# Spreading the first batch's 16 dense units over the second batch's attention steps

## The chip, the cores and the metric

The kernel runs on one core of a Trainium2 chip. The metric is device time in microseconds (us) of one execution. The engines of the core are named as in the profile: PE is the matrix engine, DVE the vector engine, ACT the activation engine, POOL the GpSimd engine, SP the engine whose queue issues nearly all DMAs; each runs its own instructions in the order in which the program lists them.

## The reference

Three stages follow one another. B is 4 batches, H 8 heads, S 576 positions, D 64.

```python
q_rot, k_rot = rotate(q), rotate(k)                    # rotary embedding
scores = q_rot @ k_rot.T / sqrt(D);  attn = softmax(scores)
x = (attn @ v)  -> [2304 tokens, 512]                  # stage 1
h = x @ w_in;  g = maximum(0.01 * h, h);  x2 = g @ w_out   # stage 2, d_ff = 2048
e = argmax_e(cos(x2, expert_emb) / tau)                # stage 3, 8 experts
out = gate * (relu(x2 @ w1[e]) @ w2[e])                # d_ff of an expert = 1024
```

Stage 2 needs whole rows of x, thus all eight heads of a token, and stage 3 needs x2 of all tokens before the last of its blocks can be formed.

## The kernel before, in words

Attention is done in 144 *steps*: 16 groups g (a batch and a pair of heads; four groups make a batch) of nine units u (128 queries of one head; the ninth takes the last 64 queries of both heads). Step i handles unit i: `a_max` (L574, DVE) reads the scores S of unit i and writes E, `a_exp` (L579, ACT) and `a_hi`/`a_lo` (L583 ACT, L587 DVE) follow for unit i-1, a DMA transposes the result P into PT, `a_pv` (L622, PE) multiplies it with v four steps later, `a_fin` (L640 to L644, DVE) normalizes, and `a_scores(i+1)` (L565, L567, L569, PE) makes the next scores. The scores have one buffer, so the scores of step i+1 wait for `a_max` of step i. Groups 0 to 3 (steps 0 to 35, batch 0) use another form in fp32.

The dense stage 2 is cut into 72 *units* in ten blocks of 256 tokens (two blocks hold 128). A unit of a 256-token block is 24 matmuls h<-x,wi (`m_s1`, L251), then on ACT and DVE `m_g` (L258), `m_leaky` (L261), `m_gh` (L265), `m_gl` (L269), then 12 matmuls into acc (`m_s2`, L281). Blocks 0 and 1 are the first 512 tokens of batch 0 and take 16 units; blocks 2 and 3 are those of batch 1, block 4 is the rest of batches 0 and 1, and so on. A block may begin once its rows have been scaled, split into two fp16 halves and transposed by DMA (`x_done`, L669 to L680). When a block's last unit has been added up, `m_out` (L293, L295) writes x2 and `route` follows for each 128 rows: a store by SP (L310), a sum of squares (L322), four transposes (L326), a copy (L329), eight small matmuls (L333) and one DVE operation (L335).

The order of all instructions is written out by hand in `step`. It walks through a string of letters; what belongs to the change:

```python
for z in ORDER_W if whole else ORDER1 if ... else ORDER_B if second else ORDER_A:
ORDER_A = 'ESXFHshLlVxsC'
ORDER_B = 'GXEKFHs2LVxsCo'
```

`S` is `m_s1` and stands only in ORDER_A, so a unit can begin only in a step of that form. If a unit was begun, or one is still between its two matmul parts, `M.second` is set and the following step takes ORDER_B, which holds the unit's `m_g` and `m_leaky` (`G`, `K`) and the `m_s2` of the unit before (`2`). `h` and `l` of ORDER_A are `m_gh` and `m_gl`. Without a pause the steps alternate A, B, A, B, and one unit begins in every second step: begun in step s, its second part stands in step s+3. `m_ready` says whether the next unit's rows and weights are there; then the unit begins as early as the order allows. `s` and `x` are slots into which background jobs (preparing the next groups, `x_done`, `route`, decoding of the weights) are put by a budget; the dense units are not counted in it.

After step 148 the attention is over; the units that are left run without attention steps, and the expert stage follows.

Of the kernel before, what the change touches and what calls it, by code (L numbers as in the profile page):

```python
# [40 lines left out]
EARLY = 2  # L41
TLOAD = 4
BUR = 1.5
ORDER_W = 'HXtEFVCsTsxs'
ORDER1 = 'HXEsFVsLsxCs'
ORDER_A = 'ESXFHshLlVxsC'
# [49 lines left out]
def attention_moe_kernel(ctx: ExitStack, tc: tile.TileContext, qkv, w_in, w_out, emb, tau, w1, w2,  # L96
# [30 lines left out]
    def ps_h():  # L127
        return psH.tile([128, 512], F32, name="h")
# [22 lines left out]
    munits = []  # L151
# [13 lines left out]
    M = Ctx()  # L165
# [5 lines left out]
    M.wdone = [set(), set()]  # L171
    M.scaled = set()
    M.step, M.tick = -1, 0
    block_of = {z: j for j, bl in enumerate(blocks) for z in bl}
    xjobs, vjobs, rjobs, wjobs = deque(), deque(), deque(), []

# [56 lines left out]
    def m_ready():  # L233
        if M.unit == len(munits):
            return False
        j, fs = munits[M.unit]
        return j < M.ready and all(f in w for f, _, _ in fs for w in M.wdone)

    def m_s1():

        if not m_ready():
            return None
        j, fs = munits[M.unit]
        M.unit += 1
        m = Ctx()
        m.j, m.fs, m.h = j, fs, ps_h()
        for f, c0, c1 in fs:
            n = 0
            for a, b_ in ((0, 0), (1, 0), (0, 1)):
                for c in range(4):  # L250
                    nc.tensor.matmul(m.h[:, c0:c1], lhsT=wi[:, a, c, 128 * f:128 * f + 128], rhs=xT[j][:, 4 * b_ + c, 0:c1 - c0],  # L251
                                     start=(n == 0), stop=(n == 11))
                    n += 1
        return m
# [808 lines left out]
    def step(i):  # L1063
# [4 lines left out]
        for e in budget:  # L1068
            budget[e] = min(budget[e] + rate[e], BUR * rate[e])
        now = i is not None and 0 <= i < n  # L1070
# [5 lines left out]
        second = M.second  # L1076
        for z in ORDER_W if whole else ORDER1 if rate is RATE1 and (turned or not m_ready()) else ORDER_B if second else ORDER_A:
            if z == "E" and whole:
# [5 lines left out]
            elif z == "t" and turned:  # L1084
                a_turned_end(*end_)
            elif z == "S":
                m = m_s1()
                M.second = bool(m or M.g or M.s)
                if m:
# [55 lines left out]
    for i in range(n + LAG + 1):  # L1145
# [4 lines left out]
        j = i - LAG - 1  # L1150
# [223 lines left out]
```

## Time and profile before

| | us |
|---|---|
| median of 3 runs | 1034.22 (1034.07 to 1034.79) |
| the profiled execution, its own time | 1036.97 |
| span from first to last instruction | 1035.2 |
| PE / DVE / ACT busy in the span | 943.6 / 776.9 / 672.0 |
| mean granted PE clock | 0.939 |

Busy shares over the whole span hide stages: the fp32 attention of batch 0 lies up to about 200 us, attention with dense units from there to about 640 us, the remaining dense units to about 762 us, and the experts after that. A gap in brackets behind a PE row is idle time before it, with what ended it.

### The profile page before, as it was taken

Reading aid. Unit: us, or ns where it says so; the run is one execution under the profiler, and the core shown is the slowest. Engines: PE = TensorE matmul, PEld = TensorE weight load, DVE = VectorE, ACT = ScalarE, POOL = GpSimd, SP = SyncE. Lnnn points to the kernel's source line nnn. Section 1 sums busy time; section 2 is a strip of 40 time slices with the busy share of each in tenths; the row PEclk is TensorE's granted clock in tenths of the full one; section 3 lists DMA queues with packets and bytes.
Section 4 is the critical chain, followed back from the end, with each engine's and each line's share of the span. In section 5 each row is a group of like instructions: output and inputs, shape, how many; then the busy total and the mean of one; then the engine's idle time right before and its main releaser. Section 6 shows DMA issues by size and latency. Waiting matters only on the chain. (4 is left out here: it accounts for less than half of the span.)

```text
span 1035.2 us, 19847 instructions
## 1 busy us (share of the span) xinstructions
PE 943.6 (91%) x7259; PEld 778.5 (75%) x7259; DVE 776.9 (75%) x1632; ACT 672.0 (65%) x1081; POOL 64.2 (6%) x64
## 2 busy tenths in 40 slices
PE   2577897999999689999899999999999999999996
PEld 1466786767787578888778888888877788888884
DVE  5776776878878878887987967422566999899992
ACT  5666666775655765765775655423255898888882
POOL 0000000000000000000000000000000452111110
PEclk9977656599999899999999999999999999999998
DMA  6334245385886787788687666200333111116190
GB/s 203 118 111 131 73 130 159 58 161 90 145 168 134 150 173 121 133 169 154 139 167 160 109 122 97 60 1 22 103 112 123 41 52 52 41 41 204 58 333 20
DMA packets 223623, 120.08 MB, mean 116 GB/s; under 512 B 194711, under 2 KB 204439, under 8 KB 223520
## 3 DMA queue, kind: packets, MB, share of 16 engines
q1 hardware_dynamic: 220320, 108.79, 45.5%
q0 software_dynamic: 3200, 9.97, 2.8%
q8 instruction: 59, 0.97, 0.4%
q14 instruction: 44, 0.36, 0.1%
HBM read 120.04 MB, written 10.49 MB: 126 GB/s over the span
## 5 line engine op out<-in xcount | busy, mean ns | idle before, releaser
L251 PEld LDWEIGHTS <-wi 128*128 128x128 f16 x1920 | 171.8, 99 | 27.1 <-issue 6.6
L281 PE MATMUL acc<-wo,gh 128*128 128x512 f32 x576 | 152.3, 406 | 2.7 <-ACT gh L265 2.7
L579 ACT ACTIVATE E<-E,amx 128x576 f32<-128x576 f32 x144 | 110.6, 768 | 32.4 <-DVE E L574 32.1
L258 ACT ACTIVATE g<-h 128x512 f32<-128x512 f32 x72 | 43.0, 598 | 133.8 <-PE h L251 57.1
L281 PEld LDWEIGHTS acc<-wo,gh 128*128 128x128 f32 x576 | 103.7, 189 | 26.4 <-ACT gh L265 4.7
L574 DVE TENSOR_SCALAR_CACHE_REDUCE E<-S,sc 128x576 f32<-128x576 f32 x108 | 87.8, 813 | 41.8 <-PE S L567 27.8
L251 PE MATMUL h<-xT,wi 128*128 128x256 f16 (+1 forms) x1152 | 113.5, 257 | 0.0
L587 DVE SCALAR_TENSOR_TENSOR P<-E,P 128x576 f16<-128x576 f32 x108 | 81.2, 752 | 17.4 <-ACT P L583 17.1
L583 ACT ACTIVATE P<-E 128x576 f16<-128x576 f32 x108 | 73.9, 684 | 31.4 <-DMA PT<-P 28.3
L251 PE MATMUL h<-xt,wi 128*128 128x256 f16 x768 | 90.8, 276 | 2.3 <-DMA xt<-x 2.3
L622 PEld LDWEIGHTS <-PT 128*128 128x128 f16 (+1 forms) x1680 | 61.1, 100 | 24.6 <-issue 14.7
L281 PE MATMUL acc<-wo,gl 128*128 128x512 f32 x288 | 77.9, 392 | 0.0
L622 PE MATMUL o<-v,PT 128*128 128x65 f16 (+3 forms) x1680 | 69.7, 194 | 6.5 <-DMA PT<-P 6.5
L261 DVE SCALAR_TENSOR_TENSOR g<-h,g 128x512 f32<-128x512 f32 x72 | 49.5, 688 | 29.2 <-ACT g L258 29.1
L565 PE MATMUL S<-stk 128*128 128x288 f16 (+1 forms) x240 | 60.9, 293 | 9.9 <-DVE E L574 9.8
L269 DVE TENSOR_TENSOR gl<-g,gh 128x512 fp32r<-128x512 f32 x72 | 49.4, 686 | 24.3 <-ACT gh L265 14.5
L622 PE MATMUL o<-v,ET 128*128 128x65 f32 (+1 forms) x400 | 64.5, 328 | 0.0
L281 PEld LDWEIGHTS acc<-wo,gl 128*128 128x128 f32 x288 | 54.7, 190 | 12.2
L622 PEld LDWEIGHTS o<-v,ET 128*128 128x128 f32 (+1 forms) x400 | 62.3, 246 | 0.7 <-issue 0.7
L989 PE MATMUL h<-w,hth 128*128 128x512 f32 x176 | 55.2, 395 | 0.4 <-ACT hth L973 0.4
L265 ACT ACTIVATE gh<-g 128x512 fp32r<-128x512 f32 x72 | 44.5, 618 | 15.1 <-PE acc L281 14.2
L550 PE MATMUL S<-qk 64*128 64x288 f32 (+1 forms) x96 | 38.5, 616 | 17.2 <-DVE ET L608 14.4
(255 smaller groups left out, 1957.5 us busy)
## 6 DMA issues: line engine op xcount, KB each, us to landing
rb<-in_w SPq DMA_DIRECT2D x78, 512.0 KB
ra<-in_w SPq DMA_DIRECT2D x76, 512.0 KB
raw<-in_qkv SPq DMA_DIRECT2D x15, 640.0 KB
raw<-in_w_in SPq DMA_DIRECT2D x16, 512.0 KB
raw<-in_w_out SPq DMA_DIRECT2D x16, 512.0 KB
x2s<-x SPq DMA_DIRECT2D x18, 256.0 KB
raw<-in_qkv SPq DMA_DIRECT2D x14, 320.0 KB
v<-v SPq DMA_DIRECT2D x12, 162.5 KB
```

The lines of the kernel that those rows point to most:

```text
L251: nc.tensor.matmul(m.h[:, c0:c1], lhsT=wi[:, a, c, 128 * f:128 * f + 128], rhs=xT[j][:, 4 * b_ + c, 0:c1 - c0], start=(n == 0), stop=(n == ...
L261: nc.vector.scalar_tensor_tensor(out=m.g, in0=m.h, scalar=0.01, in1=m.g, op0=ALU.mult, op1=ALU.max)
L265: nc.scalar.activation(out=m.gh, in_=m.g, func=AF.Copy)
L269: nc.vector.tensor_tensor(out=m.gl, in0=m.g, in1=m.gh.bitcast(F32), op=ALU.subtract)
L281: nc.tensor.matmul(M.acc[:, t], lhsT=g_[:, tt], rhs=wo[:, a, f], start=(f == 0 and n == 0), stop=(f == NF - 1 and n == 2))
L565: nc.tensor.matmul(ps[o:o + m, n, 0:288], lhsT=stk[:, h, c0:c0 + m], rhs=stk[:, 2 + h, ks], start=True, stop=False)
L574: nc.vector.tensor_scalar(out=e[:, 0:S].rearrange("p (a b) -> p a b", a=2), in0=ps[:, :, 0:288], scalar1=-0.125 if g < WHOLE else pairs[g] ...
L579: nc.scalar.activation(out=e[:, 0:S], in_=e[:, 0:S], func=AF.Exp, scale=-1.0, bias=mx)
L583: nc.scalar.activation(out=p[:, 0:576], in_=e[:, 0:S], func=AF.Copy, scale=TWO15)
L587: nc.vector.scalar_tensor_tensor(out=p[:, 576:1152], in0=e[:, 0:S], scalar=TWO15, in1=p[:, 0:576], op0=ALU.mult, op1=ALU.subtract)
L622: nc.tensor.matmul(o[ob:ob + m, 256 * h:256 * h + w], lhsT=pt[:, i, q0:q0 + m], rhs=v[:, j, h, c:c + w], start=(n == 0), stop=(n == len(to ...
L989: nc.tensor.matmul(OP[kk], lhsT=h_[:, c, :], rhs=wt[a][c // 2][:, 512 * (c % 2):512 * (c % 2) + 512], start=(n == 0), stop=(n == len(todo) ...
```

## The change

The diff gives the first batch's units a schedule. `M.first` is 16, the number of units of blocks 0 and 1. `M.begin` holds the step in which unit 0 begins. Until step 76, unit k is let through only once k (76 - begin) is no more than 16 (step - begin). Unit 16, the first of batch 1, is held to step 76 by the same line. From step 76 on nothing is held.

```diff
+NEXT = 76
...
+    M.first = sum(j < 2 for j, _ in munits)
...
         j, fs = munits[M.unit]
+        if not M.unit:
+            M.begin = M.step
+        if M.step < NEXT and M.unit * (NEXT - M.begin) > M.first * (M.step - M.begin):
+            return None
         M.unit += 1
```

No instruction is added or removed; only the order in the queues changes.

## Rows read from the trace of the kernel before

**Rows 1.** Windows: stretch, length, busy (count) of PE, PEld, DVE, ACT, POOL, clock, DMA.
```profile
203.60:244.79 41.19, 40.12 (x330) 29.06 (x329) 33.45 (x79) 27.05 (x46) 0.12 (x1) 0.97 0.72 124
244.79:296.31 51.52, 51.52 (x492) 41.06 (x492) 41.49 (x98) 31.67 (x55) 0.23 (x2) 1.00 0.68 131
296.31:334.06 37.75, 37.38 (x380) 30.95 (x378) 31.87 (x74) 22.25 (x38) 0.12 (x1) 1.00 0.79 160
334.06:370.55 36.49, 25.47 (x256) 20.35 (x257) 29.12 (x81) 26.29 (x50) 0.12 (x1) 0.86 0.76 154
370.55:384.71 14.16, 11.27 (x101) 8.93 (x100) 9.92 (x22) 7.53 (x14) 0.00 (x0) 0.88 0.89 208
384.71:640.00 255.29, 248.03 (x2600) 208.84 (x2598) 208.43 (x496) 164.35 (x282) 0.70 (x6) 1.00 0.74 137
640.00:762.00 122.00, 121.91 (x1006) 103.65 (x1005) 52.43 (x140) 42.94 (x77) 2.22 (x2) 1.00 0.22 62
```
**Rows 2.** L574 up to 355.1 us: count, ns min/median/max, first and last start.
```profile
L574 DVE TENSOR_SCALAR_CACHE_REDUCE E<-S,sc x38: 687/816/821, 199.8 to 351.3; 128x576 f32<-128x576 f32 x38
```
**Rows 3.** L251 from 199.5 to 334.0 us, same columns.
```profile
L251 PE MATMUL h<-xT,wi x384: 272/273/421, 202.6 to 329.2; 128*128 128x256 f16 x192
```
**Rows 4.** Timeline of PE (start, duration): start of the dense work, a regular pair, routing.
```profile
202.65 4.26 PE L251 MATMUL h<-xT,wi 128*128 128x256 f16 x24
...
218.98 2.79 PE L251 MATMUL h<-xT,wi 128*128 128x256 f16 x24
221.61 0.58 PE L622 MATMUL o<-v,PT 128*128 128x65 f16 x14
...
222.93 2.11 PE L281 MATMUL acc<-wo,gh 128*128 128x512 f32 x8
...
225.78 0.59 PE L622 MATMUL o<-v,PT 128*128 128x65 f16 x14
...
290.58 0.66 PE L326 MATMUL t<-idn,x 128*128 128x128 f32 x4
294.73 1.04 PE L333 MATMUL t<-enT,x2T 128*128 128x8 f32 x8
```
**Rows 5.** Timeline of PE from 336 to 380 us: three gaps and a slow row.
```profile
336.11 0.59 PE L622 MATMUL o<-v,PT 128*128 128x65 f16 x14 [2.09 <-DMA PT<-P]
...
355.19 4.45 PE L251 MATMUL h<-xt,wi 128*128 128x256 f16 x24 [2.25 <-DMA xt<-x]
...
378.62 0.28 PE L565 MATMUL S<-stk 128*128 128x288 f16 x1 [2.89 <-DVE E L574]
...
379.02 3.14 PE L281 MATMUL acc<-wo,gh 128*128 128x512 f32 x8
```
**Rows 6.** Windows around these gaps in which the clock fell, columns as in the first group.
```profile
345.00:353.00 8.00, 4.36 (x35) 3.21 (x32) 7.79 (x22) 5.66 (x12) 0.00 (x0) 0.57 0.56 107
353.00:360.00 7.00, 4.80 (x39) 3.73 (x39) 5.04 (x13) 4.72 (x9) 0.00 (x0) 0.76 0.54 109
...
378.00:385.00 7.00, 6.38 (x42) 4.86 (x42) 6.41 (x16) 5.26 (x11) 0.00 (x0) 0.76 0.79 178
```
**Rows 7.** DVE groups 203.6 to 334.06 us: count, busy, mean ns, idle before, releasers.
```profile
L574 DVE TENSOR_SCALAR_CACHE_REDUCE E<-S,sc 128x576 f32<-128x576 f32 x33 | 26.7, 810 | 19.1 <-PE S L569 12.9 <-PE S L567 5.9
L261 DVE SCALAR_TENSOR_TENSOR g<-h,g 128x512 f32<-128x512 f32 x16 | 11.0, 687 | 0.0
L269 DVE TENSOR_TENSOR gl<-g,gh 128x512 fp32r<-128x512 f32 x15 | 10.3, 684 | 0.0
```
**Rows 8.** Waits from 334.06 to 384.71 us: total, times, longest.
```profile
ACT x L674 <- DMA xt<-x: 4.9, 1, 4.9
DVE x L676 <- ACT x L674: 3.7, 1, 3.7
```
**Rows 9.** Timeline of SP: the two stores of block 1.
```profile
348.27 0.58 SPq L310 DMA_DIRECT2D x2s<-x  x1
...
368.13 0.46 SPq L310 DMA_DIRECT2D x2s<-x  x1
```

## The prediction, made before the result was known

> **What bounds the kernel now.** I read the windows first, cut where a_max of steps 37, 47, 59, 69, 77 and 80 starts, because a share over the whole span mixes stages. In the first three windows PE is busy 40.12 of 41.19, 51.52 of 51.52 and 37.38 of 37.75 us, at a clock of 0.97 to 1.00; DVE has 80 to 84% of the time [rows 1]. PE bounds there, and the DVE groups say the same from the other side: a_max waited 19.1 us in all for the scores from PE [rows 7]. In the fourth window (steps 69 to 76) PE is busy 25.47 of 36.49 us at 0.86, and in the fifth 11.27 of 14.16 at 0.88. From 384.71 to 640 us it is busy 248.03 of 255.29, and from 640 to 762 us, where only dense units are left, 121.91 of 122 [rows 1].
>
> Why the fourth window is empty is seen by counting. The first a_max with the tile sc belongs to step 36. 38 of them start up to 355.1 us, the last at 351.3, so that is step 73 [rows 2]. Unit 0 stands between the scores of steps 37 and 38: it begins in step 37, at 202.65 us [rows 4]. By 334 us, 384 matmuls of L251 have run, 24 each, so all 16 units [rows 3]: one in every second step, the last in step 67. Unit 16 starts at 355.19, in step 74, and waits 2.25 us for its rows even then [rows 5]. Between, steps 69 to 73 hold only the last second part (step 70).
>
> **The change part by part.** Nothing is added or removed: the sum is of moves. With begin 37, unit k is let through from step 37 + 39k/16 on, and it must also meet a step of form A. After a unit, A is every second step, and a refused A step is still followed by a B step, since the unit before is between its parts. So units keep to odd steps: 37, then 41, 43, 45, 47, then 51, 53, 55, 57, 59, then 63, 65, 67, 69, then 73 and 75, and unit 16 in 77. There are four pauses of one unit (steps 39, 49, 61, 71). A pause leaves two steps light for PE, not adjacent: step 39 has no first part and step 42 no second.
>
> *Price of a unit.* On PE from start to start 2.63 us for the first part (218.98 to 221.61) and 2.85 for the second (222.93 to 225.78), together 5.5 us [rows 4]. On DVE 0.687 + 0.684 us [rows 7]; back to back they overlap a little, and I take 1.2. Routing of 128 rows is 0.66 + 1.04 = 1.7 us of PE [rows 4].
>
> *Steps 37 to 46 (41.19 us).* One first and one second part fewer. PE 40.12 - 5.5 = 34.6, DVE 33.45 - 1.2 = 32.3. The bounds are 34.6 and 41.2. The first 24 matmuls ran at the low clock (4.26 us against 2.79 [rows 4]), and now a light step follows at once. I take 37.0.
>
> *Steps 47 to 58 (51.52 us).* One unit fewer, and the routing of block 0 (3.4 us of PE, about 1.2 of DVE) goes four steps later and into the next window. PE 51.52 - 5.5 - 3.4 = 42.6, DVE 41.49 - 2.4 = 39.1. Bounds 42.6 and 51.5; I take 44.0, since DVE is near.
>
> *Steps 59 to 68 (37.75 us).* PE 37.38 - 5.5 + 3.4 = 35.3, DVE unchanged at 31.9. Bounds 35.3 and 37.8; I take 36.5.
>
> *Steps 69 to 76 (36.49 us).* Units 13, 14 and 15 begin here where 16 and 17 did, and three second parts stand where one did: 2.6 + 2 x 2.85 = 8.3 us more of PE. Block 1's routing leaves (3.4), and so do its two stores of 256 KB in SP's queue, 0.58 and 0.46 us to issue [rows 9]. The slow clock costs less: the first part at 355.19 took 4.45 instead of 2.79 [rows 5], and with the rest I count 2.5. PE 25.47 + 8.3 - 3.4 - 2.5 = 27.9. DVE gets three operations more (1.8) and loses 1.2 of block 1's output and routing: 29.12 + 0.6 = 29.7. The lower bound is DVE's 29.7, the upper 36.49 + 8.3 - 3.4 = 41.4, all of it uncovered. What stalled PE was the transposes of P (2.09), the rows (2.25) and DVE [rows 5]; a dense part in front of such a wait fills it, and unit 16's rows have landed long before step 77. I take 32.5: DVE's time and a little.
>
> *From step 77 on.* Unit 16 begins in step 77 instead of 74. Units still alternate from there, so everything behind is 1.5 units late: two first parts and one second, 2 x 2.63 + 2.85 = 8.1, and block 1's routing 3.4, 11.5 us of PE, come at last to the stretch at 640 to 762 us, where PE has nothing to hide them in. Against it, the window of steps 77 to 79 has 2.9 us of idle PE and a second part at the low clock (3.14 instead of 2.11 us [rows 4, 5]); its wait starts at a transposed row that ACT waited 4.9 and DVE then 3.7 us for [rows 8], which stays. I count 1 us back.
>
> Sum: 37.0 + 44.0 + 36.5 + 32.5 = 150.0 against 166.95, 16.95 less; plus 11.5, less 1: 6.4 us less. The profiled execution took 1036.97 us (span 1035.2), so 1030.6; on the median of 1034.22 that is 1027.8.
>
> The same by lost time: the last two windows lose 13.9 us of idle PE and, at the low clock, some 4 more; 11 or 12 of these 18 would be given back at once, and 5 to 6 lost anew, mostly in the first three windows, where DVE now comes near to PE.
>
> **The rivals.**
>
> *Everything is filled.* All windows fall to their lower bounds (142.2 us) and the fifth gives back its 2.9 and 1.5: 24.75 - 11.5 + 4.4 = 17.6 less, 1016.6; with half of it between that and the forecast, about 1021. For it: a_max is what waits, not PE. Against: DVE would be busy over 90% in each.
>
> *The stalls stay.* The fourth window is as long as before with its new work hidden (36.5), and the pauses give back only what the delay takes, because DVE and ACT, not PE, set the light steps. Windows 38.5, 46.5, 37.2 and 36.5 are 158.7: 8.2 less, 11.5 more, 1 back: 1036.5; with one of the two, 1032 to 1034. For it: DVE has 29.12 of 36.49 us there, and transposed rows are waited for whatever PE does [rows 1, 8]. Against: in the windows before, PE was at 99%.
>
> [...]
>
> *The order isn't followed.* If unit 16's rows were not what holds step 74, or if a unit were held by weights, the count above would differ. The 16 units ran at every second step without a miss, so neither was; I give this no chance of its own.
>
> **How the numbers follow.** About 0.2% (2 us) is what a measurement of this kernel can tell from no change. Forecast 0.52, its own range 1024 to 1031; everything filled 0.15; stalls stay 0.22, of it 0.06 below 1032.2, 0.12 within and 0.04 above 1036.3; the clock 0.11, of it 0.03 within and 0.08 above. Faster 0.52 + 0.15 + 0.06 = 0.73, same 0.15, slower 0.12. The range takes in most of the first two rivals and the short dips: 1020.5 to 1036.
>
> **What would show it.** Right: 16 units of L251 up to about 354 us instead of 334, in groups of 1, 4, 5, 4 and 2 with longer steps between; the four windows by step at about 37, 44, 36.5 and 32.5 us, together 150; clock 1.00 from 210 us to the end of the attention; no wait for xt at unit 16; the end of the dense units 6 us earlier, though the stretch without attention is some 8 to 12 us longer. [...]

## The result: 0.63% slower, where 0.6% faster was forecast

The changed kernel takes 1040.06 us (median of 7 runs, 1037.64 to 1042.29) against 1034.22 before: ratio 1.0063, 95% interval 1.0043 to 1.0082. The forecast was 1027.8, its range ended at 1036.0: it missed the sign, and the result lies outside the range.

The profiled execution took 1040.16 us (span 1038.2). The first 36 steps, which hold the same instructions in both kernels, took 4.3 us less in this execution than in the one of before; between executions of the kernel before and of the experiments they differ by up to 5 us. So stages are compared from the a_max of step 36 on. From there to the end it is 835.4 us before and 842.7 after, 7.3 more.

Windows of the profile after, cut where a_max of steps 37, 47, 59, 69, 74, 78, 80 and 143 starts, and at the end of the last first part; columns as in [rows 1]:

```profile
199.35:240.77 41.42, 37.24 (x294) 26.12 (x293) 32.13 (x77) 25.83 (x44) 0.12 (x1) 0.89 0.63 123
240.77:286.72 45.95, 44.79 (x440) 34.55 (x440) 39.86 (x95) 27.81 (x45) 0.23 (x2) 1.00 0.72 138
286.72:323.18 36.46, 34.52 (x363) 28.74 (x361) 31.19 (x75) 24.23 (x43) 0.12 (x1) 1.00 0.76 158
323.18:348.33 25.15, 19.94 (x182) 15.51 (x181) 19.32 (x53) 15.19 (x29) 0.00 (x0) 0.86 0.80 156
348.33:371.54 23.21, 13.70 (x135) 11.02 (x135) 14.15 (x36) 11.75 (x21) 0.12 (x1) 0.87 0.73 153
371.54:381.32 9.78, 9.78 (x80) 7.66 (x80) 7.05 (x17) 6.90 (x15) 0.00 (x0) 0.79 0.67 161
381.32:633.06 251.74, 247.97 (x2600) 209.23 (x2599) 206.89 (x495) 165.02 (x284) 0.71 (x6) 1.00 0.72 138
633.06:765.57 132.51, 131.80 (x1075) 111.96 (x1074) 56.54 (x148) 45.63 (x82) 2.22 (x2) 1.00 0.23 62
```

The same cuts in the kernel before (the first three are in [rows 1]):

```profile
334.06:355.20 21.14, 10.91 (x113) 8.25 (x114) 18.59 (x52) 15.35 (x30) 0.00 (x0) 0.84 0.83 165
355.20:377.75 22.55, 19.74 (x204) 16.43 (x204) 14.08 (x37) 13.22 (x24) 0.12 (x1) 0.92 0.78 172
377.75:384.71 6.96, 6.08 (x39) 4.60 (x39) 6.37 (x16) 5.25 (x10) 0.00 (x0) 0.75 0.76 171
384.71:638.40 253.69, 246.44 (x2593) 207.54 (x2592) 206.86 (x492) 163.45 (x281) 0.70 (x6) 1.00 0.74 137
638.40:762.46 124.06, 123.97 (x1015) 105.39 (x1016) 54.45 (x145) 43.84 (x79) 2.22 (x2) 1.00 0.23 65
```

| stage | before | forecast | after |
|---|---|---|---|
| steps 37 to 46 | 41.19 | 37.0 | 41.42 |
| 47 to 58 | 51.52 | 44.0 | 45.95 |
| 59 to 68 | 37.75 | 36.5 | 36.46 |
| 69 to 73, 74 to 77, 78 and 79 | 21.14, 22.55, 6.96 | 45.7 in all | 25.15, 23.21, 9.78 |
| 80 to 142 | 253.69 | as before | 251.74 |
| dense units alone | 124.06 | 11.5 more | 132.51 |

The order is the one that was worked out: 384 matmuls of L251 (L257 in the changed file) now end at 352.3 us, where they ended at 329.2 [rows 3]. The two middle windows shrink as forecast, and the stretch without attention pays 8.45 us for the delay. But steps 69 to 79 took 58.1 us instead of 50.7, and steps 37 to 46 gave nothing. In the forecast's own cuts, steps 69 to 76 took 36.68 us (323.18 to 359.86) where 32.5 was forecast, and steps 77 to 79 took 21.46 (359.86 to 381.32) where 13.2 was.

```profile
L257 PE MATMUL h<-xT,wi x384: 269/273/421, 198.4 to 352.3; 128*128 128x256 f16 x192
```

**Step 69.** PE in the changed kernel (start, duration, in brackets the idle time before and what ended it):

```profile
322.98 2.78 PE L257 MATMUL h<-xT,wi 128*128 128x256 f16 x24
327.85 0.90 PE L628 MATMUL o<-v,PT 128*128 128x65 f16 x14 [2.09 <-DMA PT<-P]
```

The first part of unit 13 now stands in front of the wait for a transposed P. The wait is 2.09 us all the same, as long as it was without that part (336.11 us in [rows 5]), and step 69 takes 7.48 us instead of 4.86: the added 2.6 us were not hidden.

**Step 77.** Timelines of the changed kernel, first PE, then ACT, then SP:

```profile
358.73 2.78 PE L257 MATMUL h<-xt,wi 128*128 128x256 f16 x24
361.35 0.58 PE L628 MATMUL o<-v,PT 128*128 128x65 f16 x14
...
370.29 3.78 PE L287 MATMUL acc<-wo,gh 128*128 128x512 f32 x8 [7.87 <-ACT gh L271]
373.87 1.91 PE L287 MATMUL acc<-wo,gl 128*128 128x512 f32 x4
```

```profile
360.35 0.68 ACT L589 ACTIVATE P<-E 128x576 f16<-128x576 f32 x1
369.00 0.72 ACT L680 ACTIVATE x<-x,ps 128x512 f16<-128x512 f32 x1 [7.97 <-DMA xt<-x]
369.63 0.61 ACT L271 ACTIVATE gh<-g 128x512 fp32r<-128x512 f32 x1
```

```profile
354.39 3.26 SPq L516 DMA_TRANSPOSE stk<-stg  x1
359.76 1.13 SPq L524 DMA_DIRECT2D zq<-stk  x2
360.94 0.58 SPq L370 DMA_DIRECT2D raw<-in_qkv  x1
361.64 4.06 SPq L597 DMA_TRANSPOSE PT<-P  x2
365.79 1.26 SPq L686 DMA_TRANSPOSE xt<-x  x1
```

The copy at L680 writes x16, which has one buffer; it may not run before the transpose xt of the row before has read it. That transpose was issued at 365.79, last in a chain in SP's queue: stk, a wait until it has landed, zq, a 640 KB load, two PT. In the kernel before, the same copy waited 4.9 us [rows 8]. Steps 74 to 76 are faster now (11.53 us against 15.35), the chain is not, so ACT comes to the copy early and waits 8.0; and unit 15's gh, which needs no DMA, stands behind it, and behind gh stands PE. In the trace gh runs at 369.63 us, right behind the copy at 369.00 and 9.3 us after the start of the step's P at 360.35; in E9 below, where the copy is moved, gh runs 0.6 us after the start of that P (364.79 and 364.20 us). PE's last matmul ended at 362.4 us, the granted clock was 0.50 from 365.50 to 375.70, and the second part took 3.78 and 1.91 us, where the one at 354.96 us took 2.11 and 1.07.

**Steps 37 to 46.** PE, then DVE, around the first pause:

```profile
209.73 0.40 PE L571 MATMUL S<-stk 128*128 128x288 f16 x1 [2.88 <-DVE E L580]
...
211.11 3.78 PE L287 MATMUL acc<-wo,gh 128*128 128x512 f32 x8
```

```profile
207.60 0.74 DVE L682 SCALAR_TENSOR_TENSOR x<-x,ps,x 128x512 f16<-128x512 f32 x1
208.26 0.68 DVE L197 SCALAR_TENSOR_TENSOR raw<-raw 128x512 uint32<-128x512 uint32 x1
208.86 0.81 DVE L580 TENSOR_SCALAR_CACHE_REDUCE E<-S,sc 128x576 f32<-128x576 f32 x1
```

The light step 39 is no shorter (2.61 us in both kernels): its a_max stands behind x_done's and the weights' decoding in DVE's queue, and PE stands still for 2.88 us instead of running a first part. Then the clock is 0.50 from 208.5 to 215.3 us, and the next second part starts at 3.78 us instead of 2.12.

### The profile page after: what moved, and what is told of

It reads as the page before. It is cut to its first block, busy times and chain, and to the rows that moved or that the text cites. A ratio compares the mean times of both kernels' runs of the same rounds, so it can differ in the third digit from the quotient of the medians.

```text
span 1038.2 us, 19837 instructions
## 1 busy us (share of the span) xinstructions
PE 938.2 (90%) x7259; PEld 772.2 (74%) x7259; DVE 776.6 (75%) x1632; ACT 672.6 (65%) x1081; POOL 64.6 (6%) x64
## 5 line engine op out<-in xcount | busy, mean ns | idle before, releaser
L257 PEld LDWEIGHTS <-wi 128*128 128x128 f16 x1920 | 171.0, 98 | 24.4 <-issue 4.5
L287 PE MATMUL acc<-wo,gh 128*128 128x512 f32 x576 | 156.7, 415 | 15.9 <-ACT gh L271 15.8
L287 PEld LDWEIGHTS acc<-wo,gh 128*128 128x128 f32 x576 | 106.8, 195 | 41.6 <-ACT gh L271 19.1
L257 PE MATMUL h<-xT,wi 128*128 128x256 f16 (+1 forms) x1152 | 113.5, 257 | 0.0
L257 PE MATMUL h<-xt,wi 128*128 128x256 f16 x768 | 89.2, 273 | 0.0
L628 PE MATMUL o<-v,ET 128*128 128x65 f32 (+1 forms) x400 | 60.9, 316 | 0.0
L628 PEld LDWEIGHTS o<-v,ET 128*128 128x128 f32 (+1 forms) x400 | 58.7, 235 | 0.7 <-issue 0.7
L604 PE MATMUL h<-idn,E 128*128 128x128 f32 x144 | 31.8, 359 | 23.8 <-ACT E L585 23.8
```

Source lines behind the costliest of these rows:

```text
L287: nc.tensor.matmul(M.acc[:, t], lhsT=g_[:, tt], rhs=wo[:, a, f], start=(f == 0 and n == 0), stop=(f == NF - 1 and n == 2))
L628: nc.tensor.matmul(o[ob:ob + m, 256 * h:256 * h + w], lhsT=pt[:, i, q0:q0 + m], rhs=v[:, j, h, c:c + w], start=(n == 0), stop=(n == len(to ...
```

## The experiments

Each ratio is against the kernel before, in runs of the same chip; (a to b) is its 95% interval.

**E1: gh ahead of the background slot.**
```diff
-ORDER_A = 'ESXFHshLlVxsC'
+ORDER_A = 'ESXFHhsLlVxsC'
```


> The changed kernel with one letter moved: in the A steps m_gh stands ahead of the background slot on ACT instead of behind it. The dense units begin in the same steps as in the changed kernel. Theory 1 (place in ACT's queue): the 7.87 us gap of PE in step 78 came only because gh of unit 15 was queued behind a copy into x16 that waited 8.0 us for a DMA; with gh ahead, the second part of unit 15 runs during that wait, the gap is under 5 us and the kernel takes 3 to 5 us less than the changed one (about 1035 to 1037). Rival (the DMA chain): what sets steps 74 to 79 is when the transposed row lands; PE work moved into the wait is not missing afterwards, a_max of step 80 starts within 1 us of the changed kernel's (counted from step 69), and the time stays 1039 to 1041.

1039.0 us, 1.006 (1.0035 to 1.0085). The second part of unit 15 now runs inside the wait: PE has 17.16 us of work in steps 74 to 77 instead of 13.70, and steps 78 and 79 fall to 7.52. But PE then waits 5.42 us for a_max of step 78 before it can make the scores of step 79, and the stretch from step 74 to 77 is no shorter than in the changed kernel:

```profile
347.36:371.40 24.04, 17.16 (x158) 13.43 (x158) 14.15 (x36) 12.20 (x22) 0.12 (x1) 0.88 0.79 149
```
The time went the rival's way (its prediction for step 80 didn't: that came 3.3 us earlier, counted from step 69; steps 47 to 58 and 80 to 142 took 1.5 and 2.2 us more instead). The length of steps 74 to 77 does not hang on where gh stands. The edit changes every step of form A, so it says no more than that.

**E2: units in even steps.**
```diff
         if not M.unit:
+            if M.step < 38:
+                return None
             M.begin = M.step
```


> The changed kernel with unit 0 held to step 38, so that units begin in even steps: pauses at 40, 52 and 64, unit 15 in step 74, unit 16 in step 76 instead of 77. In step 77 the order is then form B, and gh of the unit before was made in step 76. Theory 1: no gap of 7.9 us in step 78, since the second part due there has its inputs; with one pause and one step less delay 5 to 9 us less than the changed kernel, 1031 to 1035. Rival (the DMA chain): the wait of ACT stays about 8 us, the parity helps only by the smaller delay of 1 step, half a unit or 2.7 us: about 1037.

1037.17 us, 1.0038 (1.0019 to 1.0056). Again the rival: steps 74 to 77 take 23.8 us, ACT waits 8.3 us for x16, and the stretch of dense units alone is 129.59 us, 2.9 less than in the changed kernel, for one step less of delay.

**E3: no pause behind unit 0.**
```diff
-            M.begin = M.step
+            M.begin = M.step - 2
```


> The changed kernel with its schedule counted from two steps earlier: units 0 to 3 follow at every second step as in the kernel before, the pauses stand at 45, 55, 63 and 73, unit 15 begins in 75 and unit 16 in 77 as in the changed kernel. Theory (clock): the first pause cost what it should have given, because the clock fell to half from 208.5 to 215.3 us; without it steps 37 to 46 take about 37 us instead of 41.4 and the kernel 3 to 5 us less than the changed one (1035 to 1037). Rival: the pause's gain is lost to DVE and ACT, which still decode weights there; then the later first pause gives no more, and the time is 1039 to 1041.

1048.13 us, 1.0152 (1.0127 to 1.0178): neither theory had that. Steps 37 to 46 are no faster (41.88 us), though the clock was 0.93 in them instead of 0.89, so the higher clock did not bring the 37 us. The window also holds one second part (2.85 us of PE) more than in the changed kernel, 306 matmuls against 294, so it does not separate the clock from DVE's queue. Steps 59 to 68 and 69 to 73 are 4.0 and 3.6 us longer than in the changed kernel. In step 60 PE waits 3.72 us for a transposed P:

```profile
287.12:327.53 40.41, 34.72 (x339) 28.36 (x338) 30.91 (x73) 23.13 (x40) 0.12 (x1) 0.92 0.71 138
327.53:356.23 28.70, 21.16 (x172) 16.32 (x170) 20.41 (x54) 17.06 (x32) 0.00 (x0) 0.85 0.71 149
```
```profile
287.00 0.59 SPq L370 DMA_DIRECT2D raw<-in_qkv  x1
287.70 0.38 SPq L316 DMA_DIRECT2D x2s<-x  x1
288.20 6.14 SPq L597 DMA_TRANSPOSE PT<-P  x2
```
A store of block 0's routing now falls right behind a group's load, and the two PT behind both take 6.14 us in SP's queue. That this is the cause was not tested.

**E4: the delay alone.** In the kernel before:
```diff
         j, fs = munits[M.unit]
+        if M.unit == 16 and M.step < 77:
+            return None
```


> The kernel before with one thing alone: unit 16 is held to step 77; the first 16 units stand as early as before, and there is no pause. If the delay of 1.5 units is paid in full in the stretch without attention (8.4 us there), and steps 74 to 79 give back some 3 us because unit 16 no longer waits for its rows: 5 us more than before, 1038 to 1041. If steps 74 to 79 get shorter by the work that left them, the time is that of the kernel before, 1033 to 1035, and the changed kernel's loss is all due to the spreading.

1040.56 us, 1.0072 (1.0049 to 1.0096). The delay is paid in full, and what leaves steps 74 to 77 does not shorten them; PE's work there falls from 19.74 to 12.99 us and the length stays:

```profile
352.45:375.13 22.68, 12.99 (x130) 11.03 (x131) 12.09 (x34) 11.53 (x22) 0.12 (x1) 0.67 0.79 171
...
633.90:766.43 132.53, 131.82 (x1075) 112.00 (x1074) 56.55 (x148) 45.62 (x82) 2.22 (x2) 1.00 0.23 62
```
The delay alone costs as much as the whole change. By now steps 74 to 77 had taken 22.6 to 24.0 us in six kernels, with 13 to 20 us of PE work in them: it is not PE's work that sets their length. The wait of the copy for x16 grew with the time that the engines came early: 4.9 us in the kernel before, 8.0 in the changed one, 9.5 in E1, 9.7 in E4.

**E5, E6, E7: zq copies out of SP's queue**, in the kernel before, the changed kernel and E2:
```diff
-                nc.sync.dma_start(out=zq[g % 2][...], ...)
+                nc.gpsimd.dma_start(out=zq[g % 2][...], ...)
```


> The kernel before with one queue changed: the two zq<-stk copies of each group, which wait in SP's queue for the transpose stk to land, are issued by POOL. Theory 2 (the DMA chain): in every kernel so far the stretch from a_max of step 74 to that of step 78 took 22.6 to 24.0 us whatever dense work stood in it, because SP issues stk, zq, raw, two PT and then the xt on which ACT waits one behind the other. Without the wait in SP's queue this stretch falls by 3 to 6 us here, and the kernel gets 2 to 5 us faster: 1029 to 1032. Rival: what takes long is the landing of the transposes beside the 640 KB load, not the queue's order; then the stretch stays 22 to 24 us and the time 1033 to 1035.

1027.84 us, 0.9922 (0.9899 to 0.9945).

> The changed kernel with the zq<-stk copies issued by POOL instead of SP. Theory 2: the stretch of steps 74 to 77 falls from 23.2 us by 4 to 8, more than in the kernel before, because here the engines came to it early and waited; the distance between the two kernels shrinks from 6 us to 2 to 4, time 1032 to 1036. Rival (landing beside the load): stretch 22 to 24 us, time 1039 to 1041.

1035.86 us, 1.0018 (1.0001 to 1.0034).

> The kernel with units in even steps (unit 16 in step 76) and the zq<-stk copies issued by POOL. If both gains add: 3.5 us (even against the changed kernel, counted on the measured medians 1037.2 and 1040) and those of the queue, 1029 to 1033, equal to the kernel before with the same queue within 2 us. If the DMA landing sets the stretch: about 1037.

1031.46 us, 0.9954 (0.9938 to 0.9971). All three get faster, but not where theory 2 said, so that E6's time, inside its range, is no support for it: steps 74 to 77 still take 22.92, 22.11 and 22.68 us. The gain lies elsewhere: in the changed kernel steps 69 to 73 fall from 25.15 to 22.25, all of it in step 69 (7.48 to 4.38), where PE no longer waits for the transposed P; in the kernel before steps 80 to 142 fall from 253.69 to 250.01. The distance between the two kernels did not shrink (0.0096 of the ratio after, 0.0063 before), and E7 stayed 0.0032 behind E5, where at most 2 us were expected.

**E8: the kernel before once more.**

> The kernel before once more, unchanged, for a second profile: how far the stages differ from one execution to the next. Expected: fp32 steps 0 to 35 up to 5 us different, since their clock changes from run to run; steps 36 to 143 within 2 us in every stretch; 22 to 24 us from step 74 to 78; 124 us without attention. If steps 69 to 73 or 74 to 77 come out as in the kernel that only holds unit 16 (24.2 and 22.7 us), then single profiles differ there by 3 us for reasons that no kernel change made.

1037.33 us, one run. From step 36 to the end 836.3 us against 835.4; no stretch differs by more than 1.1 us (steps 69 to 73: 22.27), and the first 36 steps by 0.7. E4 and E13 below have the same order up to step 76 and differ by 1.4 us in steps 69 to 73 (24.23 and 22.84). So stages of single profiles can be compared to about 1.5 us.

**E9, E10: the fifth row's copy later**, in the changed kernel and in the one before. The row with c = 4 is copied at the earliest four steps after the last transpose xt was issued, in step 80 instead of 77, and the rest of that row's preparation, its DVE operation and its transpose, follows it:
```diff
-        yield Piece(A=0.61)
+        yield Piece(A=0.61, when=lambda: c < 4 or M.tick >= M.turned + 4)
         x16 = mp.tile([128, 2 * DM], F16, name="x16", bufs=X16)
...
         nc.sync.dma_start_transpose(out=xT[j][...], in_=x16)
+        M.turned = M.tick
```


> The changed kernel with one copy moved: the fifth row of batch 1 (the one that needs x16 a second time within two steps) is copied in step 80 instead of 77, so ACT no longer stands still in step 77 behind the transpose that frees x16. Theory 3 (ACT's queue): that wait of 8.0 us alone makes step 77 take 11.7 us; without it the stretch of steps 74 to 77 falls from 23.2 to 17 to 19 us and the kernel from 1040 to 1034 to 1036. Rival (DMA latency as such): the transposes PT that step 78 needs stand behind the same 640 KB load and the same stk; PE then waits for PT instead, the stretch stays above 21 us, and the time is 1038 to 1040.

1034.37 us, 1.0011 (0.9992 to 1.0029).

> The kernel before with the same copy in step 80 instead of 77. Theory 3: its wait was 4.9 us and half hidden, so 1 to 3 us faster, 1031 to 1033, and the two kernels come nearer by 3 us or more. Rival (DMA latency): no change, 1034 to 1035.

1029.58 us, 0.9963 (0.9945 to 0.9981). Steps 74 to 77, first of E9, then of E10:

```profile
352.18:366.53 14.35, 12.70 (x134) 10.44 (x134) 13.41 (x36) 10.54 (x19) 0.12 (x1) 1.00 0.67 131
```
```profile
353.33:371.54 18.21, 17.36 (x176) 14.34 (x176) 13.41 (x37) 12.53 (x23) 0.12 (x1) 0.92 0.74 165
```
Theory 3 holds for this stretch: the copy's wait made it 8.9 us longer in the changed kernel and 4.3 in the one before. Without it the stretch is 0.9 to 2.0 us longer than PE's work in it, here and in E13, E14 and E15. The whole kernel gains less, 0.52% (5.4 us) and 0.37% (3.8 us), and the two kernels come nearer by 0.15% (1.5 us), not by the 3 us expected. A second buffer for x16 would show the same more directly; it was not tried.

**E11, E12: the 640 KB load later**, in the changed kernel and in the one before:
```diff
-        if g + 1 < 4 * B:
-            load(g + 1, 2)
         vjobs.append(Job(prep_v(g, rawv, s3)))
+        if g + 1 < 4 * B:
+            yield Piece(at=i0 + 3)
+            load(g + 1, 2)
```


> The changed kernel with the 640 KB load raw of each next group issued in step i0+3 (step 75 for the group of step 72 and so on, three to four steps later) instead of right behind stk and zq. Theory (DMA latency): the load's packets hold up the transposes behind it; without it between stk and the two PT, PT and xt land 3 to 5 us sooner, the stretch of steps 74 to 77 falls to 18 to 20 us, the gaps behind PT at the other group boundaries get smaller too, and the kernel takes 1033 to 1036. Rival (theory 3, only ACT's wait for x16): the xt behind it is still the fifth in the chain; 21 to 23 us, 1038 to 1040.

1041.68 us, 1.0081 (1.0062 to 1.01).

> The kernel before with the load raw issued three to four steps later. Theory (DMA latency): a gain here too, from the same stretch and from the waits for PT in steps 69, 87 and 105: 1029 to 1033. Rival: 1034 to 1035, the same as before.

1034.02 us, 1.0003 (0.9985 to 1.0022). The rival, in both: steps 74 to 77 stay at 23.00 and 22.74 us, and ACT waits 7.75 and 5.06 us for x16. The load is not what holds the chain. E11 lies 1.7 us above even the rival's range.

**E13, E14, E15: what is left without that wait.** E13 is E4, E14 is E2, E15 is E5, each with E9's edit.

> The kernel before with unit 16 held to step 77 and the fifth row's copy in step 80: the delay alone, without the wait for x16. If the delay is paid in full in the stretch without attention (8.4 us) and steps 74 to 77, now free to shrink, give back what left them: step 74 to 78 in 14 to 15 us, 3.5 less than the kernel before with the same copy moved (18.2), time 3 to 5 us above that kernel's 1029.6: 1033 to 1035, the same as the changed kernel with the copy moved (1034.4). Then the spreading as such gives nothing and costs nothing. Rival: the spreading pays (5.6 us in steps 47 to 58): this kernel is 3 to 6 us slower than the changed one with the copy moved, 1037 to 1040.

1036.52 us, 1.0037 (1.0021 to 1.0053). Steps 74 to 77 fall to 12.56 us with PE at 10.54, as expected, but steps 78 and 79 take 13.06 where E10 has 6.61, PE busy only 6.70 of it, because PE now stands still in step 78 for a transposed P:

```profile
357.09:369.65 12.56, 10.54 (x116) 8.85 (x116) 11.35 (x33) 11.13 (x21) 0.12 (x1) 0.86 0.69 138
369.65:382.71 13.06, 6.70 (x65) 5.25 (x66) 6.48 (x16) 5.16 (x11) 0.00 (x0) 0.74 1.03 231
```
```profile
376.01 0.94 PE L624 MATMUL o<-v,PT 128*128 128x65 f16 x14 [6.95 <-DMA PT<-P]
```
E4 had the same wait (6.91 us) beside the copy's. So where little dense work stands in these steps, E9's rival is right in part: without the copy's wait the transposes of P set the time, and steps 74 to 79 together fall by 4.5 us only. The time lies between theory and rival: 0.0026 of the ratio above E9.

> The changed kernel with units in even steps (unit 16 in step 76, one step less delay) and the fifth row's copy in step 80. If what is left of the loss is the delay: 2.8 us less in the stretch without attention than the changed kernel with the copy moved, 1030 to 1033. Rival (steps 69 to 73 are set by the chain of DMAs, whatever is saved): no gain from the parity, 1034 to 1035.

1032.86 us, 1.0000 (0.9982 to 1.0018), inside the range of the delay's theory, and dense units alone take 128.89 us, 2.8 less than in E9, as it had it. But steps 74 to 79 take 3.5 us more (27.68 against 24.19), and the two ratios differ by less than their intervals: a gain in the whole is not shown.

> The kernel before with both repairs: the zq<-stk copies issued by POOL and the fifth row's copy in step 80; the dense units stand as early as they can. If both gains add (1034.4 - 7 - 4.3): 1022 to 1026. Rival: both shorten the same chain of DMAs in steps 74 to 77, so only part adds: 1026 to 1028.

1025.84 us, 0.9934 (0.9908 to 0.9961). The median lies in the range for gains that add, but this chip was faster for the kernel before as well (1033.13 us against 1034.89 in E5's runs); by its ratio E15 is no better than E5 (0.9922), so the two repairs do not add measurably. E5 and E15 both beat the kernel before and the changed one, and both begin the dense units as early as they can.

## Why the prediction was wrong

The schedule, the price of a unit, the two middle windows (forecast 80.5 us together, measured 82.4), the rows of unit 16 that no longer wait, and that units after 77 come late were right. The misses, against the forecast of 6.4 less:

- *Steps 37 to 46: 4.4 us.* "I take 37.0"; it was 41.42. A light step is worth something only if the next scores' a_max is not itself late. DVE still had x_done and the decoding in its queue, so PE stood still where its dense part had been, and behind unit 0 the clock was 0.50 from 208.5 to 215.3 us. The price was 2.88 us of gap and some 2 of slow matmuls (3.78 instead of 2.12 us and 1.38 instead of 1.07). This is read from the trace: no experiment separates the two (E3 does not).
- *Steps 47 to 58: 2 us* (45.95 against 44.0).
- *Steps 69 to 79: 58.1 us where 45.7 was forecast, 12.4 us.* This is the step that failed: that PE's gaps there are room for dense work, because "a dense part in front of such a wait fills it", and that the wait for the transposed row "stays" at 4.9 us and gives 1 back. In step 69 a first part stands in front of the wait, and the wait is 2.09 us as before; E6, which takes SP's wait for stk out of its queue, removes it. In step 77 the wait for the row is not of fixed length: it ends when a transpose has landed, and whoever comes earlier waits longer, 8.0 us here. E4 shows it by taking PE work away, E1 by moving PE work in: the stretch stays. E9 shows which wait it is: 8.9 us go with it in the changed kernel, against 4.3 before. Which link of the chain in SP's queue sets the landing in step 77 is open: neither the wait for stk alone (E5 to E7) nor the load alone (E11, E12) does.
- *The delay: 8.45 us in the stretch of dense units, 8.1 expected for the units themselves.* The 3.4 us of routing did not arrive there; steps 80 to 142 took in that and gave 1.95 more, as their 7.2 us of idle PE fell to 3.8. That is 5 us better than forecast, an error that happened to help: without it the forecast would have been 18.8 us off.

4.4 + 2 + 12.4 - 5 = 13.8, and 7.3 - (-6.4) = 13.7.

By length and granted clock of the windows above, PE had about 26 us at half clock in steps 37 to 79, against about 16 before (an estimate: twice the length times what the clock lacks to 1.00, since the low stretches show 0.50, as 208.5 to 215.3 us does here and 346 to 352 us before). Part of that time PE stood still and lost nothing by it; what the rest cost was not isolated.

What the change is worth without the wait: with the copy moved, E10 is the kernel before, E13 the delay alone, E9 delay and spreading, at 0.9963, 1.0037 and 1.0011. So the delay costs about 0.74% (7.6 us), the wait for P in E13's step 78 included, and spreading returns about 0.26% (2.7 us), hardly more than the two intervals leave open; with the wait in place E4 and the changed kernel, 1.0072 and 1.0063, can't be told apart. The rival "the stalls stay" (1036.5) had the right sign and most of the mechanism: steps 69 to 76 took 36.68 us where it has 36.5. It had too small a chance, a stall of fixed length in step 77 where the measured one grew, and 3.6 us too little; the range, up to 1036.0, stopped just short of it. What a dip in a pause costs, which the chance of 0.11 for the clock and the short dips in the range need, is shown by no run; of the four pauses, those of steps 39 and 71 had a dip, 0.57 over 8 and over 4 us, and those of steps 49 and 61 had none, 1.00 from 240.77 to 323.18 us.

Of the 4 us more in steps 69 to 73 (25.15; the kernel before showed 21.14 and 22.27), 2.6 lie in step 69, and E6 takes them away with SP's wait for stk. Open: the rest, which is no more than single profiles differ by, and the 9.1 us of step 60 in E3.

## What to carry to other kernels

An idle stretch of the bounding engine is room for moved work only if the stretch's end depends on that engine. Before moving work into it, follow the wait that ends last back to a DMA or a buffer; where it ends at one, taking work out of the stretch does not shorten it (steps 74 to 77: the engines came earlier and waited longer), work put in front of the wait is not hidden by itself (step 69), and here the work held back was paid in full where PE has no gaps (8.45 us). In a kernel with such a saturated tail, work that can begin early should begin early (E10 against E9), and one copy that waits for a DMA should not stand on the same engine ahead of what the critical engine needs (step 77: ACT waits 7.97 us at the copy, and PE 7.87 us for the gh behind it).

## What was not expected of the hardware

The clock fell in two of the four pauses: 0.57 from 208 to 216 us (step 39) with PE counted busy 6.27 of 8.00 us, and 0.57 from 338 to 342 us (step 71), but it was 1.00 throughout steps 47 to 68 with two pauses of the same kind. It fell also behind the wait of step 69, where PE is counted busy 3.96 of 4.00 us, so the busy share does not tell it. After the long gap of step 77 it was 0.50 for about 10 us:

```profile
208.00:216.00 8.00, 6.27 (x19) 4.01 (x19) 6.42 (x12) 4.65 (x7) 0.00 (x0) 0.57 0.81 159
328.00:332.00 4.00, 3.96 (x25) 2.82 (x23) 2.99 (x9) 3.15 (x7) 0.00 (x0) 0.58 0.99 212
338.00:342.00 4.00, 3.40 (x9) 2.75 (x10) 3.93 (x9) 2.76 (x6) 0.00 (x0) 0.57 0.44 82
365.50:375.70 10.20, 5.41 (x14) 3.92 (x15) 3.95 (x9) 3.18 (x5) 0.00 (x0) 0.50 0.73 155
```
And 20 small copies (80 KB each) that waited in SP's queue were worth 0.8% of the kernel (E5); in step 69 of E6 the transposed P that stands behind them came in time.
